# A mixture of experts after linear attention on one core: in which order two sums of the upper right product are split into high and low parts

## The chip, the cores and the metric

The kernel runs on one core of a Trainium2 chip. The metric is the device time of one execution in microseconds (us). Runs are compared by their median. The engines are named as the profile names them: PE (matmuls) with PEld (its weight loads), DVE (the vector engine), ACT (the scalar engine), POOL (GpSimd) and SP (which issues DMAs).

## What is computed

The reference is a decayed linear attention, whose output is the input of a mixture of eight experts. Cut to what matters here:

```python
state = gamma * state + einsum('bhd,bhe->bhde', k[:, :, t], v[:, :, t])
y[:, :, t] = scale * einsum('bhd,bhde->bhe', q[:, :, t], state)
x = y as rows of 512 values, 3072 of them
logits = x @ w_gate + log1p(exp(x @ w_noise)) * noise
for e in range(8):
    for k in range(2):                      # each row goes to two experts
        mask = top2[:, k] == e
        h = np.maximum(x[mask] @ w1[e], 0.0)
        out[mask] += top2_w[mask, k, None] * (h @ w2[e])
```

## The kernel before

The attention comes first (some 115 us), then the experts, one after the other. This document is about the experts 1 to 7, counted in the order in which they run (expert 0 is treated otherwise). Each has a table of slots for its rows (tokens): 832 for the experts 1 to 3, 800 for 4 and 5, 768 for 6 and 7. Every fp32 value is held as two fp16 values, a high and a low part, so that one product takes three matmuls (high by high, high by low, low by high).

**First layer of an expert (`mm1s`).** The product of w1 (1024 features) with the rows is cut into 2 by 2 blocks, halves of the inner dimension and of features by halves of the slots, and done with seven block products in place of eight, as Strassen and Winograd do. A block product is made for 128 features at a time: six matmuls over half of the slots (416, 400 or 384 columns). Such a piece is called a slot of the program, and `mm1s` counts them 0 to 27 (`slot[0]`; to keep them apart from the table's slots, they are "pieces" from here on). Pieces 0 to 11 make the first half of the features (`i = 0`), pieces 12 to 25 the second, with the last two products of the first half at 14 and 15, and 26 and 27 close. What lies in PSUM after a piece is taken up by one of three helpers:

- `kept` (L911): ACT copies it to a tile s1, s2 or s5 in SBUF. The matmuls that add to the same bank afterwards wait for that copy: piece 17 (S2 by T2) adds to the bank of piece 12, so it waits for the copy of piece 12.
- `added` (L915): DVE adds a bank to such a tile. When both of its 128 features are in (`u` is 1), `parts` follows.
- `parts` (L907, L908): ACT writes the high part (with the Relu) at once, and DVE writes the low part one piece later, out of the list `wait`.

s1 is the product's first slots (`n0 == 0`), s2 and s5 the other slots (`n0 == half`). s2 is the upper right block. Its last sum comes with piece 10 of the first half and with piece 24 of the second, that of s1 one piece later, with 11 and 25. The pieces are in program order on every engine, and an engine's queue keeps that order. Between the pieces `hook` puts other work into the queues: at pieces 5, 7, 9 and 11 ACT's high parts of w2 (`w_hi`, L214), at 6, 8, 10 and 12 DVE's low parts of w2 (`w_lo`, L219), at 11 the gates' scales (`out_scale`, L948 to L957, which waits for POOL's fetches of gates, L690), at 14, 16, 18 and 20 ACT's sums of squares (L190), at 26 a scale (L193, L200).

**Second layer (`second`, `mm2`).** For each block of 128 rows 24 matmuls of 512 columns (L992, L993, L994 for each of eight groups of 128 features, in order) run over h, the split features. Block 0 lies in the first slots. Its groups 2 and 3 are the last s1, so that its seventh matmul (L992, group 2) waits for the high part of s1, and its ninth (L994) for the low part of s1. The other slots are first read by block 3, 72 matmuls after the start.

```python
for u in range(2):
    product("S4", "B22", c[u], f0 + u, added(s2, u, f0, half), False)
product("A12", "B21", bank("pR"), f0 + 1, added(s1, 1, f0, 0))
```

Of the kernel before, what the change touches and what calls it, by code (L numbers as in the profile page):

```python
# [95 lines left out]
def moe_kernel(ctx, tc, qT, kT, kt, vt, noise, wgn, w1, w2, ctab, qtab, xbuf, gbuf, out):  # L96
# [143 lines left out]
    def a_part(n):  # L240
        return [WT["s" + h][:, int(n[1]) - 1] if n[0] == "S" else WT["1" + h][:, 2 * int(n[1]) + int(n[2]) - 3] for h in "hl"]
# [87 lines left out]
    for i in range(2):  # L329
        u = loads.tile([128, HP, 128], F32, name=f"U{i}", bufs=1)  # L330
# [493 lines left out]
    def part(e, tag="xr"):  # L824
        pool = work if tag == "xr" else hp
        return pool.tile([128, 2, CAP // 2], F32, name="s", tag=tag, bufs=3)[:, :, :CAPS[e] // 2]

    def b_part(e, n):
        if n[0] == "T":
            i = int(n[1]) - 1  # L830
            return XT[e][:, i, 0], XT[e][:, i, 1]
        k, m = 2 * (int(n[1]) - 1), CAPS[e] // 2
        t = m * (int(n[2]) - 1)
        return [XE[e][:, h + k:h + k + 2, t:t + m] for h in (0, KT)]
# [27 lines left out]
    def s_steps(n):  # L862

        a11, a12, a21, a22 = [a_stage(1, i, j) for i in range(2) for j in range(2)]
        if n == "S1":
            XS["t"] = hp.tile([128, 2, 2, 512], F32, name="xt")
        t0, t1 = XS["t"][:, 0], XS["t"][:, 1]
        out, x, y, op = {"S1": (t0, a21, a22, OP.add), "S2": (t1, t0, a11, OP.subtract),
                         "S4": (t0, a12, t1, OP.subtract), "S3": (t1, a11, a21, OP.subtract)}[n]
        hi, lo = a_part(n)  # L870
        sc = ST["1", 1][2][:, 0:1]
        return (lambda: nc.vector.tensor_tensor(out, x, y, op=op),
                lambda: nc.scalar.activation(hi, out, AF.Copy, scale=sc),
                lambda: nc.vector.scalar_tensor_tensor(lo, out, sc, hi, op0=OP.mult, op1=OP.subtract))

    def mm1s(e, hook):

        slot = [0]
        wait = []
        half = CAPS[e] // 2  # L880

        def flush():
            while wait:
                wait.pop(0)()

        def product(a, b, p, f, then, start=True):
            (ah, al), (bh, bl) = a_part(a), b_part(e, b)
            p = p[:, :half]
            for k in range(2):
                wh, wl = [w[:, k, f * 128:(f + 1) * 128] for w in (ah, al)]  # L890
                nc.tensor.matmul(p, wh, bh[:, k, :], start=start and k == 0, stop=False, skip_group_check=True)  # L891
                nc.tensor.matmul(p, wh, bl[:, k, :], start=False, stop=False, skip_group_check=True)  # L892
                nc.tensor.matmul(p, wl, bh[:, k, :], start=False, stop=(k == 1), skip_group_check=True)  # L893
            todo = list(wait)
            del wait[:]
            then(p)
            for w in todo:
                w()
            hook(slot[0])
            slot[0] += 1  # L900

        def bank(tag):
            return psum.tile([128, 512], F32, name="pH", tag=tag, bufs=2 if tag == "pA" else 1)

        def parts(src, fs, n0):
            hi, lo = [h[:, fs, n0:n0 + half] for h in (hh, hl)]
            nc.scalar.activation(hi, src, AF.Relu)  # L907
            wait.append(lambda: nc.vector.scalar_tensor_tensor(lo, src, 0.0, hi, op0=OP.max, op1=OP.subtract))  # L908

        def kept(s, u):  # L910
            return lambda p: nc.scalar.activation(s[:, u], p, AF.Copy)  # L911

        def added(s, u, f0, n0):
            def then(p):
                nc.vector.tensor_tensor(s[:, u], p, s[:, u], op=OP.add)  # L915
                if u:
                    parts(s, slice(f0, f0 + 2), n0)
            return then

        last = []  # L920
        for i in range(2):
            f0 = 2 * i
            A, Cc = [("pA", "pA"), ("pX", "pU")][::1 - 2 * i]
            a = [bank(t) for t in A]
            s1, s2, s5 = [part(e) for _ in range(3)]
            for u in range(2):
                product("A11", "B11", a[u], f0 + u, kept(s1, u))
            for u, (q, f) in enumerate(last):
                product("A22", "T4", q, f, lambda p, f=f: parts(p, 4 + f, 0), False)
            product("A12", "B21", bank("pR"), f0, added(s1, 0, f0, 0))  # L930
            for u in range(2):
                product("S2", "T2", a[u], f0 + u, kept(s2, u), False)
            c = [bank(t) for t in Cc]
            for u in range(2):
                product("S1", "T1", c[u], f0 + u, kept(s5, u))
            for u in range(2):
                product("S3", "T3", a[u], f0 + u, added(s5, u, 4 + f0, half), False)
            for u in range(2):
                product("S4", "B22", c[u], f0 + u, added(s2, u, f0, half), False)
            product("A12", "B21", bank("pR"), f0 + 1, added(s1, 1, f0, 0))  # L940
            last = [(a[u], f0 + u) for u in range(2)]
        for q, f in last:
            product("A22", "T4", q, f, lambda p, f=f: parts(p, 4 + f, 0), False)
        flush()
# [158 lines left out]
    s2, s4, s3 = s_steps("S2"), s_steps("S4"), s_steps("S3")  # L1103
# [81 lines left out]
    for e in range(1, E):  # L1185
        more = e + 1 < E

        def hook(s):
            if s == 3:
                own_tail()  # L1190
            if e == 1 and s < 3:
                xs1(1)
            n = s - 4
            if n == 0:
                w_scale(e, "2")
            if n in (1, 3, 5, 7):
                w_hi(e, "2", n // 2)
            if n in (2, 4, 6, 8):
                w_lo(e, "2", n // 2 - 1)
            if s == 11:  # L1200
                out_scale(e, 0, len(blocks(e)))
            if more:
                if 2 <= s < 9:
                    ahead(e + 1, ((6, 0, 3, 1, 4, 2, 5)[s - 2],))
                if s in (14, 16, 18, 20):
                    w_sum(e + 1, "1", s // 2 - 7)
                if s == 26:
                    w_scale(e + 1, "1")

        mm1s(e, hook)  # L1210
        for n, t in enumerate(blocks(e)):
            if more:
# [129 lines left out]
```

## Time and profile before

| | us |
|---|---|
| median of 3 runs | 650.31 (650.27 to 653.07) |
| the profiled execution, its own time | 646.82 |
| its span, first to last instruction | 645.0 |
| between the two, outside the span | 1.82 |
| granted TensorE clock, mean over the span | 0.994 of 2.4 GHz |

The profile is of one execution, whose own time is 3.49 us under the median of the timed runs. The table gives the whole; where in it the change acts is read from the trace: the timeline (instructions in order of time, with the idle time of the engine before each and what ended it) at the middle and the end of each `mm1s`.

### The profile page before, as it was taken

The page shows a single profiled execution, that of the slowest core. Times are in us where ns is not written, and L with a number is a line of the kernel's source. Part 1 is how long each engine was busy: PE and PEld are TensorE (multiplying, and loading weights), DVE is VectorE, ACT ScalarE, POOL GpSimd, SP SyncE. Part 2 cuts the span into 40 slices and gives each one's busy share as a digit, 9 for nine tenths or more (in the row PEclk, how much of TensorE's full clock was granted, in tenths as well). Part 3 has the DMA queues.
Part 4 walks back from the last instruction along what each step waited for, and adds up shares of the span by engine and source line. Part 5 has one row for each costly group of instructions (what it writes and reads, how often), then busy time and mean ns, then how long its engine had stood idle before and what let it go on. Part 6 is the DMA issues. An engine that isn't in the chain of part 4 may idle for free.

```text
span 645.0 us, 12857 instructions
## 1 busy us (share of the span) xinstructions
PE 620.2 (96%) x4949; PEld 385.9 (60%) x4949; DVE 447.8 (69%) x947; ACT 393.0 (61%) x655; POOL 396.0 (61%) x279
## 2 busy tenths in 40 slices
PE   8999998899989999999999999999999999999995
PEld 5888887656746544654465446544654465445784
DVE  5668987577758798378937983798369746967730
ACT  4787977753446775576557655775576567656311
POOL 3556998244668844784588358736773686485164
PEclk9999999899999999999999999999999999999998
DMA  9999999953976596459745964695469646943043
GB/s 318 345 373 407 373 382 337 310 192 91 168 106 160 98 262 175 47 108 232 200 52 117 227 183 53 105 259 164 51 112 245 163 49 119 232 44 40 7 53 44
DMA packets 107392, 112.88 MB, mean 175 GB/s; under 512 B 64512, under 2 KB 84224, under 8 KB 103744
## 3 DMA queue, kind: packets, MB, share of 16 engines
q1 hardware_dynamic: 86080, 84.29, 44.3%
q0 software_dynamic: 20528, 26.90, 26.6%
q8 instruction: 40, 0.66, 0.4%
q10 hardware_dynamic: 720, 0.84, 0.4%
q14 instruction: 24, 0.20, 0.1%
HBM read 72.16 MB, written 26.47 MB: 153 GB/s over the span
## 4 chain that ended last, share of the span: by engine, by line
PE 77%; DVE 9%; DMA 4%; ACT 3%; issue 3%; POOL 2%; SPq 2%; another core or an unknown queue 0%; POOLq 0%; DVEq 0%; ACTq 0%
PE pO L994 10%; PE pO L992 10%; PE pO L993 10%; PE pH L891 9%; PE pH L893 9%; PE pH L892 9%; PE pA L366 3%; PE pY L379 3%; PE pY L385 2%; DMA xe<-xg 2%; PE pX L419 2%; PE pO L983 2%; PE pO L981 1%; PE pO L982 1%; DVE h L908 1%
## 5 line engine op out<-in xcount | busy, mean ns | idle before, releaser
L968 POOL DMA_INDIRECT out<-ot,idx x108 | 196.2, 1816 | 148.1 <-ACT ot L962 60.7
L994 PE MATMUL pO<-w2h,h 128*128 128x512 f16 x336 | 127.4, 379 | 2.3 <-DVE h L908 2.0
L992 PE MATMUL pO<-w2h,h 128*128 128x512 f16 x336 | 127.4, 379 | 2.0 <-ACT h L818 1.7
L993 PE MATMUL pO<-w2l,h 128*128 128x512 f16 x336 | 127.3, 379 | 0.0
L915 DVE TENSOR_TENSOR s<-pH,s 128x416 f32<-128x416 f32 (+2 forms) x84 | 47.4, 572 | 50.0 <-PE pH L893 28.2
L690 POOL DMA_INDIRECT gx<-gbuf,idx x54 | 60.0, 1111 | 27.8 <-issue 13.1
L680 POOL DMA_INDIRECT xg<-xbuf,idx x55 | 59.4, 1080 | 23.1 <-issue 15.4
L190 ACT ACTIVATE junk<-wst 128x1024 bf16<-128x1024 f32 x64 | 67.8, 1060 | 0.0
L907 ACT ACTIVATE h<-s 128x832 f16<-128x832 f32 (+2 forms) x42 | 36.4, 873 | 42.9 <-DVE s L915 26.8
L962 ACT ACTIVATE ot<-pO,gse 128x512 f32<-128x512 f32 (+2 forms) x48 | 32.6, 681 | 44.5 <-PE pO L994 40.1
L911 ACT ACTIVATE s<-pH 128x416 f32<-128x416 f32 (+2 forms) x84 | 40.3, 509 | 31.5 <-PE pH L893 30.4
L994 PEld LDWEIGHTS <-h 128*128 128x128 f16 x336 | 32.9, 98 | 44.4 <-DVE h L908 4.4
L992 PEld LDWEIGHTS <-h 128*128 128x128 f16 x336 | 32.9, 98 | 41.4 <-ACT h L818 2.0
L891 PE MATMUL pH<-xt,wsh 128*128 128x416 f16 (+2 forms) x168 | 56.0, 333 | 0.2 <-DVE h L908 0.2
L893 PE MATMUL pH<-xt,wsl 128*128 128x416 f16 (+2 forms) x168 | 56.0, 333 | 0.0
L892 PE MATMUL pH<-xt,wsh 128*128 128x416 f16 (+2 forms) x168 | 56.0, 333 | 0.0
L993 PEld LDWEIGHTS <-h 128*128 128x128 f16 x336 | 32.9, 98 | 38.3
L849 ACT ACTIVATE xt<-s 128x832 f16<-128x832 f32 (+2 forms) x28 | 24.5, 874 | 35.3 <-DVE s L848 35.0
L219 DVE SCALAR_TENSOR_TENSOR w2l<-wst,wsc,w2h 128x1024 f16<-128x1024 f32 x28 | 35.8, 1278 | 14.1 <-ACT w2h L214 12.1
L339 POOL TENSOR_TENSOR vp<-in_v,ct 128x512 f32<-128x512 f32 x24 | 25.1, 1046 | 29.6 <-issue 10.3
L908 DVE SCALAR_TENSOR_TENSOR h<-s,h 128x832 f16<-128x832 f32 (+2 forms) x42 | 41.3, 990 | 1.0 <-ACT h L907 0.8
L373 DVE TENSOR_TENSOR am<-pA,ct 128x512 f32<-128x512 f32 x48 | 30.8, 683 | 15.4 <-PE pA L366 12.8
(216 smaller groups left out, 1489.6 us busy)
## 6 DMA issues: line engine op xcount, KB each, us to landing
wst<-w SPq DMA_DIRECT2D x28, 1024.0 KB
in_q<-qT SPq DMA_DIRECT2D x24, 256.0 KB
in_k<-kT SPq DMA_DIRECT2D x24, 256.0 KB
in_v<-vt SPq DMA_DIRECT2D x24, 256.0 KB
xbuf<-xr SPq DMA_DIRECT2D x24, 256.0 KB
out<-zero SPq DMA_DIRECT2D x12, 512.0 KB
in_kt<-kt SPq DMA_DIRECT2D x20, 256.0 KB
wst<-w SPq DMA_DIRECT2D x8, 512.0 KB
```

The lines of the kernel that those rows point to most:

```text
L190: nc.scalar.activation(junk, st[:, i * 1024:(i + 1) * 1024], AF.Square, accum_out=ss[:, i:i + 1])
L680: nc.gpsimd.indirect_dma_start(out=x[:p1], out_offset=None, in_=xbuf[:128 + rows], in_offset=bass.IndirectOffsetOnAxis(ap=idx[:p1, i:i + 1 ...
L690: nc.gpsimd.indirect_dma_start(out=GX[e][:, t, :], out_offset=None, in_=gbuf[:128 + rows], in_offset=bass.IndirectOffsetOnAxis(ap=idx[:, i ...
L891: nc.tensor.matmul(p, wh, bh[:, k, :], start=start and k == 0, stop=False, skip_group_check=True)
L892: nc.tensor.matmul(p, wh, bl[:, k, :], start=False, stop=False, skip_group_check=True)
L893: nc.tensor.matmul(p, wl, bh[:, k, :], start=False, stop=(k == 1), skip_group_check=True)
L908: wait.append(lambda: nc.vector.scalar_tensor_tensor(lo, src, 0.0, hi, op0=OP.max, op1=OP.subtract))
L915: nc.vector.tensor_tensor(s[:, u], p, s[:, u], op=OP.add)
L968: nc.gpsimd.indirect_dma_start(out=out[s], out_offset=bass.IndirectOffsetOnAxis(ap=idx[:n, i:i + 1], axis=0), in_=ot[:n, s * HD:(s + 1) * ...
L992: nc.tensor.matmul(p, a, WT["2h"][:, f, :], start=(f == 0), stop=False)
L993: nc.tensor.matmul(p, a, WT["2l"][:, f, :], start=False, stop=False)
L994: nc.tensor.matmul(p, c, WT["2h"][:, f, :], start=False, stop=(f == FT - 1))
```

## The change

At piece 10 (and 24) the sum of s2 is no longer split at once. It is put on a list, `held`. At piece 11 (and 25) s1 is split first, and s2 right behind it: ACT's high part of s1, then that of s2, and one piece later DVE's low part of s1, then that of s2. Nothing else changes; no instruction is added or taken away.

```diff
--- before.py
+++ after.py
@@ -910,12 +910,18 @@
         def kept(s, u):
             return lambda p: nc.scalar.activation(s[:, u], p, AF.Copy)
 
-        def added(s, u, f0, n0):
+        def added(s, u, f0, n0, hold=False):
             def then(p):
                 nc.vector.tensor_tensor(s[:, u], p, s[:, u], op=OP.add)
-                if u:
+                if u and hold:
+                    held.append((s, slice(f0, f0 + 2), n0))
+                elif u:
                     parts(s, slice(f0, f0 + 2), n0)
+                    while held and n0 == 0:
+                        parts(*held.pop())
             return then
+
+        held = []
 
         last = []
         for i in range(2):
@@ -936,7 +942,7 @@
             for u in range(2):
                 product("S3", "T3", a[u], f0 + u, added(s5, u, 4 + f0, half), False)
             for u in range(2):
-                product("S4", "B22", c[u], f0 + u, added(s2, u, f0, half), False)
+                product("S4", "B22", c[u], f0 + u, added(s2, u, f0, half, True), False)
             product("A12", "B21", bank("pR"), f0 + 1, added(s1, 1, f0, 0))
             last = [(a[u], f0 + u) for u in range(2)]
         for q, f in last:
```

On ACT, at the middle of expert 2's `mm1s`. The three L907 are the high parts of s5, s2 and s1 (s_3901, s_3900 and s_3899), L214 is a high part of w2, and the two L911 at the end are the copies of pieces 12 and 13. Before:

```order
L907 ACTIVATE h2_2282<-s_3901 128x2x416
L214 ACTIVATE w2h_110<-wst2_3595,wsc2_3597 128x1024
L907 ACTIVATE h2_2282<-s_3900 128x2x416
L907 ACTIVATE h2_2282<-s_3899 128x2x416
L214 ACTIVATE w2h_110<-wst2_3595,wsc2_3597 128x1024
L911 ACTIVATE s_4051<-pH_4049 128x416
L911 ACTIVATE s_4051<-pH_4050 128x416
L907 ACTIVATE h2_2282<-pH_3897 128x416
```

Now:

```order
L907 ACTIVATE h2_2282<-s_3901 128x2x416
L214 ACTIVATE w2h_110<-wst2_3595,wsc2_3597 128x1024
L907 ACTIVATE h2_2282<-s_3899 128x2x416
L907 ACTIVATE h2_2282<-s_3900 128x2x416
L214 ACTIVATE w2h_110<-wst2_3595,wsc2_3597 128x1024
L911 ACTIVATE s_4050<-pH_4048 128x416
L911 ACTIVATE s_4050<-pH_4049 128x416
L907 ACTIVATE h2_2282<-pH_3897 128x416
```

The high parts of s2 and s1 have changed places. The L214 and the two copies stand behind both, as before.

On DVE, at the same place. L915 is the last sum of s1, L908 the low parts (of s_3900, which is s2, of s_3899, which is s1, then of a bank of piece 14), L219 a low part of w2. Before:

```order
L915 TENSOR_TENSOR s_3899<-pH_4030,s_3899 128x416
L908 SCALAR_TENSOR_TENSOR h2_2282<-s_3900,h2_2282 128x2x416
L948 TENSOR_TENSOR i2_4041<-wsc1_3191,wsc2_3597 128x1
L955 TENSOR_TENSOR gm_4044<-gx_3607,pm_2894 128x7x6
L956 TENSOR_REDUCE gsm_4045<-gm_4044 128x7
L957 TENSOR_SCALAR gse_4043<-gsm_4045,i2_4041 128x7
L908 SCALAR_TENSOR_TENSOR h2_2282<-s_3899,h2_2282 128x2x416
L219 SCALAR_TENSOR_TENSOR w2l_111<-wst2_3595,wsc2_3597,w2h_110 128x1024
L908 SCALAR_TENSOR_TENSOR h2_2282<-pH_3897,h2_2282 128x416
```

Now:

```order
L915 TENSOR_TENSOR s_3899<-pH_4029,s_3899 128x416
L954 TENSOR_TENSOR i2_4040<-wsc1_3191,wsc2_3597 128x1
L961 TENSOR_TENSOR gm_4043<-gx_3607,pm_2894 128x7x6
L962 TENSOR_REDUCE gsm_4044<-gm_4043 128x7
L963 TENSOR_SCALAR gse_4042<-gsm_4044,i2_4040 128x7
L908 SCALAR_TENSOR_TENSOR h2_2282<-s_3899,h2_2282 128x2x416
L908 SCALAR_TENSOR_TENSOR h2_2282<-s_3900,h2_2282 128x2x416
L219 SCALAR_TENSOR_TENSOR w2l_111<-wst2_3595,wsc2_3597,w2h_110 128x1024
L908 SCALAR_TENSOR_TENSOR h2_2282<-pH_3897,h2_2282 128x416
```

The low part of s2 stood ahead of the four instructions of `out_scale`; now it stands behind them and behind the low part of s1. The numbers of lines have grown by 6 from there on.

On DVE, at the end of expert 2's `mm1s`, with the last sum of s1 (into s_4051, now s_4050), the low parts and the first instruction of the next scale. Before:

```order
L915 TENSOR_TENSOR s_4052<-pH_4112,s_4052 128x416
L915 TENSOR_TENSOR s_4051<-pH_4159,s_4051 128x416
L908 SCALAR_TENSOR_TENSOR h2_2282<-s_4052,h2_2282 128x2x416
L908 SCALAR_TENSOR_TENSOR h2_2282<-s_4051,h2_2282 128x2x416
L200 TENSOR_REDUCE s1_4178<-pL_106 128x1
```

Now:

```order
L915 TENSOR_TENSOR s_4051<-pH_4112,s_4051 128x416
L915 TENSOR_TENSOR s_4050<-pH_4158,s_4050 128x416
L908 SCALAR_TENSOR_TENSOR h2_2282<-s_4050,h2_2282 128x2x416
L908 SCALAR_TENSOR_TENSOR h2_2282<-s_4051,h2_2282 128x2x416
L200 TENSOR_REDUCE s1_4178<-pL_106 128x1
```

The two low parts have changed places; nothing else moved.

## Rows read from the trace of the kernel before

**Rows 1.** The page's first part: busy time, share of the span, instructions.

```profile
PE 620.2 (96%) x4949; PEld 385.9 (60%) x4949; DVE 447.8 (69%) x947; ACT 393.0 (61%) x655; POOL 396.0 (61%) x279
```

**Rows 2.** PE's waits: engine, line, waited for; us in total, times, longest.

```profile
PE pO L994 <- DVE h L908: 2.0, 5, 0.6
...
PE pO L992 <- ACT h L907: 0.3, 1, 0.3
```

**Rows 3.** Timeline, end of expert 2: start, us, engine, line, what [idle before <-releaser].

```profile
290.76 0.95 POOL L690 DMA_INDIRECT gx<-gbuf,idx  x1 [0.30 <-issue]
...
291.83 0.59 DVE L915 TENSOR_TENSOR s<-pH,s 128x416 f32<-128x416 f32 x1 [1.69 <-PE pL L193]
...
292.33 2.08 DVE L908 SCALAR_TENSOR_TENSOR h<-s,h 128x832 f16<-128x832 f32 x2
...
292.45 0.90 ACT L907 ACTIVATE h<-s 128x832 f16<-128x832 f32 x1 [1.38 <-issue]
...
293.50 0.38 PE L992 MATMUL pO<-w2h,h 128*128 128x512 f16 x1
293.71 0.38 PE L993 MATMUL pO<-w2l,h 128*128 128x512 f16 x1
...
294.47 0.39 PE L994 MATMUL pO<-w2h,h 128*128 128x512 f16 x1 [0.37 <-DVE h L908]
```

**Rows 4.** The same, end of expert 6.

```profile
543.95 0.94 POOL L690 DMA_INDIRECT gx<-gbuf,idx  x1 [0.30 <-DVE h L908]
...
544.89 0.56 DVE L915 TENSOR_TENSOR s<-pH,s 128x384 f32<-128x384 f32 x1 [1.14 <-PE pH L893]
...
545.48 0.84 ACT L907 ACTIVATE h<-s 128x768 f16<-128x768 f32 x1 [2.73 <-DVE s L915]
...
546.34 0.56 DVE L915 TENSOR_TENSOR s<-pH,s 128x384 f32<-128x384 f32 x1 [0.89 <-PE pH L893]
```

**Rows 5.** Timeline of PE, end of expert 7.

```profile
606.63 0.27 PE L982 MATMUL pO<-w2l,h 128*128 128x256 f16 x1
606.94 0.28 PE L983 MATMUL pO<-w2h,h 128*128 128x256 f16 x1
```

**Rows 6.** Timeline, middle of expert 2.

```profile
277.18 0.95 POOL L680 DMA_INDIRECT xg<-xbuf,idx  x1 [0.31 <-issue]
...
277.66 1.01 DVE L908 SCALAR_TENSOR_TENSOR h<-s,h 128x832 f16<-128x832 f32 x1
...
277.78 0.90 ACT L907 ACTIVATE h<-s 128x832 f16<-128x832 f32 x1 [0.80 <-DVE w2l L219]
278.58 1.13 ACT L214 ACTIVATE w2h<-wst,wsc 128x1024 f16<-128x1024 f32 x1
279.62 0.91 ACT L911 ACTIVATE s<-pH 128x416 f32<-128x416 f32 x2
...
280.46 0.34 PE L891 MATMUL pH<-xt,wsh 128*128 128x416 f16 x1
```

**Rows 7.** ACT by shapes, experts 1 to 7: count, busy us, mean ns of one.

```profile
L911 ACT ACTIVATE s<-pH 128x416 f32<-128x416 f32 x36 | 17.7, 522 | 13.2 <-PE pH L893 12.2 <-issue 1.0
```

**Rows 8.** Timeline, middle of expert 4.

```profile
408.26 0.88 ACT L911 ACTIVATE s<-pH 128x400 f32<-128x400 f32 x2
...
408.85 0.33 PE L891 MATMUL pH<-xt,wsh 128*128 128x400 f16 x1
```

**Rows 9.** Timeline, middle of expert 6.

```profile
534.68 0.85 ACT L911 ACTIVATE s<-pH 128x384 f32<-128x384 f32 x2
...
535.20 0.32 PE L891 MATMUL pH<-xt,wsh 128*128 128x384 f16 x1
```

**Rows 10.** Timeline, middle of expert 1.

```profile
214.69 0.17 DVE L955 TENSOR_TENSOR gm<-gx,onef 128x7 f32<-128x7 f32 x1 [0.83 <-DMA gx<-gbuf,idx]
...
218.00 0.34 PE L891 MATMUL pH<-xt,wsh 128*128 128x416 f16 x1 [0.16 <-DVE h L908]
```

## Prediction

> **What bounds the kernel now.** I read the page first: PE is busy for 96% of the span, the other engines for 60 to 70% [rows 1]. So an edit that adds and removes no work changes the time only where PE waits. The list of PE's waits came next: in the experts 1 to 7 there is one wait that speaks of the split features, L994 for DVE's low part, 5 times, 2.0 us in all, and L992 for ACT's high part, once, 0.3 us [rows 2]. These are the matmuls of group 2 in block 0, behind the last sum of s1. The idle time shown is too small: a record of these matmuls lasts 0.38 us, while undisturbed they start 0.21 us apart (L992 at 293.50, L993 at 293.71), so each wait costs PE 0.17 us more than shown. In expert 2, L994 starts 0.76 us behind L993, a loss of 0.55 for a shown 0.37 [rows 3]. All six together: 2.3 + 6 x 0.17 = 3.3 us. That is all that a faster way from s1's last sum to its low part can win there, and 0.2 more in expert 7, where the matmuls are half as wide, 0.11 us apart, and L983 starts 0.31 behind L982 [rows 5].
>
> The timeline came last, at the two places where the change acts. It is done twice in each of seven experts: at the middle of the first layer (pieces 10 to 17) and at its end (pieces 24 to 27 and the start of the second layer).
>
> **The end of the first layer: little is won directly.** The aim on paper is that s1's low part no longer stands behind that of s2 on DVE. Look at what it waits for. In expert 2 the last sum (L915) starts at 291.83. ACT's high part of s1 follows at 292.45 and takes 0.90, to 293.35. Meanwhile DVE does the low part of s2, from 292.33; two low parts in a row take 2.08 there, 1.0 each, so that of s2 ends at 293.35, when the high part of s1 does [rows 3]. The low part of s2 was hidden by the wait for the high part. Without it DVE would idle for that 1.0 us, and s1's low part would start at the same moment. Removed: nothing. What goes behind it (low part of s2, then the scale and the low parts of groups 6 and 7) comes 1.0 us later, and ACT's high parts of groups 6 and 7 some 0.8. Group 6 is needed 12 matmuls behind the waiting one, 12 x 0.21 = 2.5 us, and the next expert's weights, whose scale is late too, a whole second layer later; both cover it. The other slots' features are read first by block 3, 72 matmuls or 15 us in.
>
> **The middle of the first layer: a new wait.** Here ACT is the engine to watch. In expert 2 it does the high part of s1 at 277.78, after 0.80 of waiting for the sum, then without a pause L214 at 278.58 and the copies of pieces 12 and 13 at 279.62 [rows 6]. The high part of s2 had been done before that, in time when ACT had nothing else. Now it stands between the high part of s1 and L214, and pushes L214 and both copies by one step of such an instruction, 278.58 - 277.78 = 0.80. A copy takes 0.52 [rows 7], so the first ends at 280.14 now and at 280.94 then. PE's piece 17 starts at 280.46, and its first matmul needs that copy [rows 6]. The cover is 0.32, less the 0.04 that passes from a copy's end to PE's start (expert 6: 534.68 + 0.48 to 535.20 [rows 9]; the 0.48 is a copy of 384 columns, estimated from 0.52 for 416 by width). PE then stands still for 0.80 + 0.04 - 0.32 = 0.52 us. For the narrower experts the step and the copy are estimated from these by width:
> - 1, 2 and 3 (416 columns): 0.52 each.
> - 4 and 5 (400): the step is 0.77, a copy 0.50; it ends at 408.26 + 0.50, and piece 17 starts at 408.85, a cover of 0.09 [rows 8]: 0.77 + 0.04 - 0.09 = 0.72 each.
> - 6 and 7 (384): piece 17 starts as the copy allows it already [rows 9], so the whole step counts: 0.74 each.
>
> Sum: 3 x 0.52 + 2 x 0.72 + 2 x 0.74 = 4.48 us.
>
> On DVE the low part of s2 moves behind `out_scale`. In expert 1 that waits for fetched gates until 214.69 [rows 10], and the low part of s2 filled that wait; it now comes behind it, and all that follows comes 1.0 later. Among it is the low part of piece 14's bank, for which piece 19 waits today, at 218.00 [rows 10]. So expert 1 loses 1.0 and not 0.52. In the other experts `out_scale` does not wait; DVE's queue then loses at most the 0.80 by which L214, and so the low weights behind it, come later, and piece 19 has the time of pieces 17 and 18 to cover that. Together: 4.48 + 0.48 = 4.96, and less the 0.2 of expert 7, whose end wait is swallowed because its PE is late by more than that: **4.8 us** is lost if the waits at the end of experts 2 to 6 stay as long as they are.
>
> **How much of that the waits at the end swallow.** PE's later arrival helps nobody at 291.83 if that release is fixed in time, and then the wait behind it shrinks by as much as PE is late. If it moves with PE, the wait stays. What ends DVE's idle 1.69 us there is unclear: the sum needs piece 25 alone, and the releaser that is named, L193, comes in PE's order a whole piece behind it [rows 3]. No row shows what it is, so I bound it: none of the 3.3 us swallowed gives +4.8, all of it +1.5. The nearest row is POOL's fetch of gates: 290.76 + 0.95 = 291.71 in expert 2, and 543.95 + 0.94 = 544.89 in expert 6, where the first late sum starts at 544.89 [rows 3, 4]; in the other three the pair fits less exactly. POOL's queue does not hang on piece 17, so the fixed end is the nearer. I take two thirds swallowed, 2.2 us: 4.8 - 2.2 = **+2.6 us**. The profiled execution would take 646.8 + 2.6 = 649.4; the median of the runs shown stands 3.5 above it, and with the same step goes from 650.3 to 652.9. That is 0.4%; a measurement of this kernel can tell 0.5%, some 3.25 us, from no change.
>
> **The rivals.**
> - *Nothing is swallowed* (0.30). The late sums are late by a fixed time behind PE's pieces, and so are late again. For it: the second late sum of expert 6 comes 1.45 behind the first [rows 4], so one release does not explain both. Against it: the fit with POOL. Then +4.8, 655.1, slower. A branch of it: in expert 2 the sum of piece 24 is on time today and would come into the late stretch with PE 0.5 later; that would cost up to another 1.45, the same distance.
> - *The new wait doesn't show* (0.10). If ACT took up the high part of s2 within time it now idles, or the copies were not on PE's way, all stays, 650.3 +- 1. Against it: the queue is in order, and ACT has no pause from 277.78 on.
> - *Faster* (0.05): ACT's high part of s2 is what holds the second late sum. In expert 6 it runs from 545.48 for 0.84, to 546.32, and the sum starts at 546.34 [rows 4]. With nothing between the two sums the second would start at 545.45, 0.89 sooner, and the waits at the end would go: -3.5 us, 646.8. It decides only if piece 17 does not wait; if that wait comes, the two together give +1.5, within the range.
> - *DVE blocked by POOL* (0.03): the moved low part, with both inputs in SBUF, meets a POOL transfer and stands still behind it. POOL's fetch lasts 0.95 [rows 6]; one such stop in each expert adds up to 7 x 0.95 = 6.7 us, of which the two pieces between 17 and 19 cover most; at worst 655.5. Against it: in expert 2 the low part of s2 starts at 277.66, while POOL's fetch runs from 277.18 to 278.13, and it takes its usual 1.01 [rows 6]. The Trainium skill, "SBUF — State Buffer", section "Who interferes with whom", says that a vector instruction with two SBUF inputs contends with a GpSimd instruction that reads SBUF, and that the second one to issue fully blocks. By that rule this start would have been held for half a microsecond; the trace does not agree for this kind of POOL instruction.
>
> **How the numbers follow.** The forecast has 0.52, and its own range is +1.5 to +3.7; the part of it above 3.25 is about a fifth. Same: 0.42 of it, the rival without the wait 0.10, a little of the others 0.03: 0.55. Slower: 0.40. Faster: 0.05. The range takes in the bounds +1.5 and +4.8, half of the rival without the wait below and the branch of the first rival above: 650.2 to 655.8; what is left out is the faster case, the other half of no wait, and the worst of the rest, under 0.2.
>
> **What would show it.** Right: in the middle of each expert the copies of pieces 12 and 13 start 0.74 to 0.80 later behind the high part of s1, piece 17 starts late by 0.5 to 0.74, named as waiting for ACT's L911; in expert 1 piece 19 waits longer for DVE's low part. At the end the low part of s1 starts right behind the high part of s1, with DVE idle before it, and not sooner after the sum. The list of PE's waits has L994 for DVE below 2.0 if part is swallowed. Wrong: piece 17 in step, or L994's wait gone with the sums of pieces 24 and 25 sooner than before; or the waits as long as ever, and the loss near 5 us.

## The result and the profile after

The changed kernel takes 654.32 us in the median of 12 runs (648.70 to 660.12), the kernel before 648.40 in 12 runs of its own (645.82 to 653.07). The ratio is 1.0067, 95% interval 1.0038 to 1.0095: slower by 4.3 us (2.5 to 6.2). The ratio leaves out the two slowest executions (659.71 and 660.12 us, at the lowest granted clock of the 12, 0.988), so it says less than the 5.9 us between the two medians. The first profiled execution of the changed kernel is the one of 659.71 us, so its span (657.9) is not compared; from it come only rows inside an expert. A second trace of the same kernel (run after_again, 649.66 us, span 647.9) gives the sums.

Engine totals of that second trace, beside [rows 1]. The counts are the same, so no work came or went. Where the loss lies these totals don't tell (PE's busy time is 1.9 us longer too, at a granted clock of 0.990 for 0.994); the waits below do:

```profile
PE 622.1 (96%) x4949; PEld 386.9 (60%) x4949; DVE 450.6 (70%) x947; ACT 392.2 (61%) x655; POOL 401.3 (62%) x279
```

PE's waits of the second trace (engine, line, waited for; us in total, times, longest), beside [rows 2]:

```profile
PE pH L891 <- DVE h L908: 3.9, 1, 3.9
...
PE pH L891 <- ACT s L911: 3.3, 7, 0.6
```

The second row is new: seven waits for ACT's copy, one in each expert. It is the first matmul of piece 17, and no other. A record lasts 0.34 us and these matmuls start 0.175 apart undisturbed, so each wait is 0.17 longer than shown: 3.3 + 7 x 0.17 = 4.5 us. The first trace has the row with the same three numbers. The row above it is expert 1's piece 19, told below. The waits of L994 (now L1000) for the low part of s1 and of L992 (now L998) for its high part have no row in this trace. They have rows in the first trace after, and longer ones in all than in [rows 2]:

```profile
PE pO L998 <- ACT h L907: 2.6, 2, 2.0
...
PE pO L1000 <- DVE h L908: 1.7, 4, 0.5
```

ACT's timeline in the middle of expert 2, first trace after, beside [rows 6] (start, us, engine, line, what [idle before <-releaser]):

```profile
285.23 1.68 ACT L907 ACTIVATE h<-s 128x832 f16<-128x832 f32 x2 [2.88 <-DVE s L915]
286.81 1.13 ACT L214 ACTIVATE w2h<-wst,wsc 128x1024 f16<-128x1024 f32 x1
287.85 0.90 ACT L911 ACTIVATE s<-pH 128x416 f32<-128x416 f32 x2
```

and PE's, the same stretch:

```profile
287.74 0.34 PE L893 MATMUL pH<-xe,w1l 128*128 128x416 f16 x1
288.40 0.34 PE L891 MATMUL pH<-xt,wsh 128*128 128x416 f16 x1 [0.33 <-ACT s L911]
```

ACT now idles 2.88 us ahead of the first high part, and then does two in a row (the "x2" of 1.68 us). The first copy starts 2.62 us behind the start of the high part of s1, where it stood 1.84 behind [rows 6]: 0.78 later. PE, which would have started piece 17 at 287.91, starts at 288.40.

DVE's timeline at the end of the first layer in expert 2, first trace after, beside [rows 3]:

```profile
298.31 0.59 DVE L915 TENSOR_TENSOR s<-pH,s 128x416 f32<-128x416 f32 x1 [0.73 <-PE pH L893]
299.07 0.59 DVE L915 TENSOR_TENSOR s<-pH,s 128x416 f32<-128x416 f32 x1 [0.17 <-PE pH L893]
300.63 1.96 DVE L908 SCALAR_TENSOR_TENSOR h<-s,h 128x832 f16<-128x832 f32 x2 [0.96 <-ACT h L907]
```

DVE idles 0.96 us for the high part of s1. The low part of s1 starts 1.56 us behind the start of the last sum and, at 1.0 us, ends 2.6 behind it. In [rows 3] it ended at 292.33 + 2.08 = 294.41, 2.58 behind the start of the sum: the same, though the last two sums start 0.76 us apart here and 2.27 apart there. What that distance does is told under the experiments.

### The profile page after: what moved, and what is told of

It is laid out like the page before. It is cut to its first block, busy times and chain, and to the rows that moved or that the text cites. A ratio compares the mean times of both kernels' runs of the same rounds, so it can differ in the third digit from the quotient of the medians.

```text
span 657.9 us, 12857 instructions
## 1 busy us (share of the span) xinstructions
PE 625.9 (95%) x4949; PEld 388.6 (59%) x4949; DVE 448.4 (68%) x947; ACT 391.8 (60%) x655; POOL 398.8 (61%) x279
## 4 chain that ended last, share of the span: by engine, by line
PE 71%; DVE 13%; ACT 5%; issue 3%; DMA 3%; POOL 2%; another core or an unknown queue 0%; SPq 0%; POOLq 0%; DVEq 0%; ACTq 0%
PE pO L1000 9%; PE pO L998 9%; PE pO L999 9%; PE pH L891 7%; PE pH L893 7%; PE pH L892 7%; PE pY L379 2%; PE pA L366 2%; PE pY L385 2%; DMA out<-ot,idx 2%; POOL out L974 2%; DVE am L373 2%; PE pT L1013 2%; ACT w2h L214 1%; ACT h L907 1%
## 5 line engine op out<-in xcount | busy, mean ns | idle before, releaser
L974 POOL DMA_INDIRECT out<-ot,idx x108 | 200.4, 1856 | 155.7 <-ACT ot L968 63.0
L998 PE MATMUL pO<-w2h,h 128*128 128x512 f16 x336 | 128.2, 382 | 2.6 <-ACT h L907 2.6
L1000 PE MATMUL pO<-w2h,h 128*128 128x512 f16 x336 | 128.2, 381 | 1.7 <-DVE h L908 1.7
L915 DVE TENSOR_TENSOR s<-pH,s 128x416 f32<-128x416 f32 (+2 forms) x84 | 47.1, 571 | 54.0 <-PE pH L893 39.8
L680 POOL DMA_INDIRECT xg<-xbuf,idx x55 | 57.7, 1049 | 25.1 <-issue 15.2
L907 ACT ACTIVATE h<-s 128x832 f16<-128x832 f32 (+2 forms) x42 | 35.2, 868 | 56.0 <-DVE s L915 46.1
L911 ACT ACTIVATE s<-pH 128x416 f32<-128x416 f32 (+2 forms) x84 | 40.2, 508 | 36.4 <-PE pH L893 33.1
L1000 PEld LDWEIGHTS <-h 128*128 128x128 f16 x336 | 33.0, 98 | 43.6 <-DVE h L908 4.1
L998 PEld LDWEIGHTS <-h 128*128 128x128 f16 x336 | 33.2, 99 | 42.5 <-ACT h L907 4.2
L908 DVE SCALAR_TENSOR_TENSOR h<-s,h 128x832 f16<-128x832 f32 (+2 forms) x42 | 40.4, 990 | 7.9 <-ACT h L907 7.9
L219 DVE SCALAR_TENSOR_TENSOR w2l<-wst,wsc,w2h 128x1024 f16<-128x1024 f32 x28 | 35.8, 1278 | 14.1 <-ACT w2h L214 10.0
```

Source lines behind the costliest of these rows:

```text
L680: nc.gpsimd.indirect_dma_start(out=x[:p1], out_offset=None, in_=xbuf[:128 + rows], in_offset=bass.IndirectOffsetOnAxis(ap=idx[:p1, i:i + 1 ...
L974: nc.gpsimd.indirect_dma_start(out=out[s], out_offset=bass.IndirectOffsetOnAxis(ap=idx[:n, i:i + 1], axis=0), in_=ot[:n, s * HD:(s + 1) * ...
L998: nc.tensor.matmul(p, a, WT["2h"][:, f, :], start=(f == 0), stop=False)
L1000: nc.tensor.matmul(p, c, WT["2h"][:, f, :], start=False, stop=(f == FT - 1))
```

## Experiments

The runs came in three groups of four. Those of a group share a chip and the runs of the kernel before. Two theories stood at first: A, that the loss is made by ACT's order in the middle of the first layer; B, that it is made at the end. A third question was what the waits at the end are, since the forecast let them swallow part of the loss.

All times in us are against the kernel before in the same group. The last four columns are from each run's one trace, worked out from the starts of PE's matmuls: what piece 17 loses in all experts (0.1, which the kernel before loses too, is given as 0); what pieces 18 to 22 of expert 1 lose; what block 0 of the second layer loses in all experts; and the time from expert 1's first matmul to the end of the span.

| run, group | ratio (95%) | us | 17 | expert 1 | block 0 | expert 1 to end |
|---|---|---|---|---|---|---|
| before, first trace | | | 0 | 0.3 | 3.6 | 448.0 |
| after, first trace | 1.0067 (1.0038 to 1.0095) | +4.3 | 4.5 | 0 | 5.2 | |
| first_half, 1 | 1.0050 (1.0005 to 1.0094) | +3.2 | 4.5 | 4.0 | 1.9 | 453.5 |
| second_half, 1 | 0.9957 (0.9923 to 0.9991) | -2.8 | 0 | 0.3 | 3.4 | 447.6 |
| low_only, 1 | 1.0034 (1.0001 to 1.0068) | +2.2 | 0 | 7.0 | 2.5 | 454.0 |
| early_hold, 1 | 0.9965 (0.9939 to 0.9991) | -2.3 | 0 | 0 | 0 | 444.2 |
| after_again, 2 | 1.0065 (1.0037 to 1.0094) | +4.2 | 4.5 | 5.7 | 0 | 452.2 |
| after_w_later, 2 | 1.0005 (0.9978 to 1.0031) | +0.3 | 0 | 5.0 | 0 | 449.3 |
| x_late, 2 | 0.9975 (0.9948 to 1.0001) | -1.6 | 0 | 5.1 | 0.2 | 447.5 |
| early_scale, 2 | 0.9900 (0.9864 to 0.9936) | -6.5 | 0 | 0 | 0 | 442.2 |
| before_again, 3 | 1.0016 (0.9983 to 1.0049) | +1.0 | 0 | 0 | 3.3 | 446.8 |
| scale_late, 3 | 1.0077 (1.0048 to 1.0106) | +5.0 | 0 | 0 | 7.8 | 450.8 |
| after_scale, 3 | 1.0048 (1.0010 to 1.0085) | +3.1 | 4.5 | 0 | 2.4 | 450.4 |
| early_scale_2, 3 | 0.9974 (0.9942 to 1.0006) | -1.7 | 0 | 0 | 1.2 | 443.6 |

**The change in the first half alone (first_half), and in the second alone (second_half).** The two edits to the changed kernel:

```diff
-                product("S4", "B22", c[u], f0 + u, added(s2, u, f0, half, True), False)
+                product("S4", "B22", c[u], f0 + u, added(s2, u, f0, half, i == 0), False)    # first_half
+                product("S4", "B22", c[u], f0 + u, added(s2, u, f0, half, i == 1), False)    # second_half
```

> The change is made in the first half of the features alone (i = 0, the middle of the first layer); the end is as before. Theory A (ACT's high part of s2 stands ahead of L214 and of the copies of pieces 12 and 13): the whole loss of the change is here. PE's piece 17 starts 0.49 us late in experts 1 to 3, 0.71 in 4 and 5, 0.79 in 6 and 7 (4.5 us in all), named as waiting for ACT's copy L911, and the time is about 4.5 us above the kernel before, 0.7%, or 2.5 to 4.5 if the waits at the end take some of it up. Theory B (the loss comes from the end, where s2's split is held behind that of s1): no more than 1 us above the kernel before.

> The change is made in the second half of the features alone (i = 1, the end of the first layer); the middle is as before. Theory A: piece 17 does not wait; at the end the low part of s1 starts where the high part of s1 ends, with DVE idle before it, and not sooner after the last sum than before. Time within 1 us of the kernel before. Theory B: 3 to 4.5 us above the kernel before. Third possibility, that the edit does at the end what it says (s1 ready sooner): 2 to 3 us below.

The half in the middle is slower by 3.2 us, the half at the end faster by 2.8. Theory B falls: the end does not lose. Added up, the halves give +0.4, and the whole change is +4.3; with intervals of these widths that is not clear of the noise, and no run here explains it. In first_half's list of waits the row of the copies reads as in the second trace after: 3.3 us, 7 times.

The gain of second_half is outside theory A's "within 1 us" at its middle, though not at its interval's end (-5.0 to -0.6). Where it can come from is seen in the traces of all runs, from the starts of the sums. With the order of before, the low part of s1 ends 2.42 to 2.58 us behind the start of the last sum when the two last sums are 1.4 us or more apart, and up to 3.02 (416 columns) when they follow each other at 0.5, for then ACT's high part of s2 and DVE's low part of s2 are both still ahead of s1's. With s2 held it is 2.41 to 2.58 in every expert of every trace (the runs with the early split apart). So the edit wins up to 0.44 us an expert at the end where the sums come close together; seven times that is 3.1 us at most. That second_half won its time there is not shown: in its own trace block 0 still loses 3.4, for 3.6 in the kernel before, and from expert 1 to the end it is 0.4 us shorter.

**Only DVE's order (low_only).** ACT's order is that of before:

```diff
-            wait.append(lambda: nc.vector.scalar_tensor_tensor(lo, src, 0.0, hi, op0=OP.max, op1=OP.subtract))
+            low = lambda: nc.vector.scalar_tensor_tensor(lo, src, 0.0, hi, op0=OP.max, op1=OP.subtract)
+            if hold:
+                held.append(low)
+                return
+            wait.append(low)
+            while held and n0 == 0:
+                wait.append(held.pop())
```

> ACT keeps its order of before (high part of s2 at pieces 10 and 24, that of s1 one piece later); only DVE's two low parts change places, in both halves. Theory A: piece 17 is in step, since nothing is added ahead of ACT's copies; what is left is expert 1, where DVE's low part of s2 moves behind the wait of out_scale, up to 0.5 us. Time within 1 us of the kernel before. Rival, that DVE's order makes the loss (the low part of a bank of piece 14, and piece 19 behind it, come 1 us later): waits of piece 19 for DVE in most experts, 3 to 5 us above the kernel before.

Piece 17 is in step in all experts, as theory A has it. The time is not within 1 us: +2.2 (0.1 to 4.4). In the trace piece 19 is late by 0.10, 0.40, 0.16 and 0.16 in experts 4 to 7, 0.8 together; in the changed kernel PE comes to piece 19 later, and this does not show. The rest is expert 1, whose pieces 19 to 22 lose 7.0 us there. DVE's timeline of low_only in expert 1:

```profile
216.84 0.17 DVE L963 TENSOR_TENSOR gm<-gx,onef 128x7 f32<-128x7 f32 x1 [5.00 <-DMA gx<-gbuf,idx]
...
217.38 1.95 DVE L910 SCALAR_TENSOR_TENSOR h<-s,h 128x832 f16<-128x832 f32 x2
219.25 1.28 DVE L219 SCALAR_TENSOR_TENSOR w2l<-wst,wsc,w2h 128x1024 f16<-128x1024 f32 x1
220.45 0.58 DVE L910 SCALAR_TENSOR_TENSOR h<-pH,h 128x416 f16<-128x416 f32 x1
```

out_scale waits 5.0 us for the fetched gates; behind it stand both low parts, the low part of w2, and only then the low part of piece 14's bank, for which piece 19 waits. In [rows 10] that wait of out_scale is 0.83. How long it is depends on how far POOL is behind PE when expert 1 is reached: the runs with out_scale at piece 11 lose 0 to 7.0 us there, and x_late, which has the order of before in the middle, 5.1. So most of the 7.0 is probably not the edit's, though no run tells the two apart. The edit adds the low part of s2, 0.94, behind the wait.

**The first 128 features of s1 split early (early_hold).** In the second half, behind second_half's edit:

```diff
+                if f0 == 2 and n0 == 0:
+                    parts(s[:, u:u + 1], slice(f0 + u, f0 + u + 1), n0)
+                    while u and held:
+                        parts(*held.pop())
+                    return
```

> Second half alone: the first 128 features of s1 are split right behind their own last sum (piece 16), so that behind piece 25 only 128 are left, in half the time each, and s2 is split behind them. 14 more instructions on ACT and on DVE over the run. If the waits of group 2 in the second layer are what the late last sum and the split behind it (0.9 us high, 1.0 us low) make, then the waits for ACT's high part and DVE's low part in block 0 are nearly gone (of some 3.3 us under 1 left) and the time is 2 to 3.5 us below the kernel before, 0.3 to 0.5%. If the late sums are late by more than the 2 us that this gives, part of the waits stays and 0 to 2 us are won.

Its list of waits has no row for block 0 in experts 1 to 7, and the time is 2.3 us lower, as expected. So the edit takes the waits at the end out of its trace, which from expert 1 to the end is 3.8 us shorter than that of before. That the timed executions pay these waits is not shown by it: second_half, with 3.4 us of them in its trace, is as fast (-2.8).

**The changed kernel again (after_again), and with the copies brought forward (after_w_later).** The second is the test of theory A that leaves the change in place. w2's last high part goes behind the copies of pieces 12 and 13, its low part to piece 16:

```diff
-            if n in (1, 3, 5, 7):
-                w_hi(e, "2", n // 2)
-            if n in (2, 4, 6, 8):
-                w_lo(e, "2", n // 2 - 1)
+            if n in (1, 3, 5, 9):
+                w_hi(e, "2", min(n // 2, 3))
+            if n in (2, 4, 6, 12):
+                w_lo(e, "2", min(n // 2 - 1, 3))
```

> The changed kernel once more, for a second trace of it. Theory A (the loss is ACT's, at the middle): piece 17 starts 0.49 us late in experts 1 to 3, 0.71 in 4 and 5, 0.79 in 6 and 7, as in the first trace; the waits at the end differ from trace to trace, since the sums there come late by 0 to 3 us. Time 2 to 4.5 us above the kernel before.

> The changed kernel, but the last high part of w2 (L214), which stands ahead of the copies of pieces 12 and 13 on ACT, is put behind them, and its low part on DVE from piece 12 to piece 16. s2 stays behind s1 everywhere. Theory A (only the copies' lateness on ACT costs): the copies come 1.04 us sooner, piece 17 is in step again in all experts, its 4.5 us are gone, and the time is within 2 us of the kernel before (ACT's backlog is 0.8 us longer than in the kernel before, and may cost 0.2 to 0.4 at piece 21 in experts 4 to 6). Rival (the order s1 then s2 itself costs, on DVE or by the late features): still 3 to 4.5 us above the kernel before.

ACT and PE in the middle of expert 2, with the copies brought forward:

```profile
278.26 1.69 ACT L907 ACTIVATE h<-s 128x832 f16<-128x832 f32 x2 [2.88 <-DVE s L915]
279.85 0.90 ACT L911 ACTIVATE s<-pH 128x416 f32<-128x416 f32 x2
280.64 1.15 ACT L214 ACTIVATE w2h<-wst,wsc 128x1024 f16<-128x1024 f32 x1
...
280.76 0.34 PE L893 MATMUL pH<-xe,w1l 128*128 128x416 f16 x1
280.94 0.34 PE L891 MATMUL pH<-xt,wsh 128*128 128x416 f16 x1
```

The two high parts still stand one behind the other, the copies follow at once, and piece 17 starts 0.18 us behind its predecessor. Theory A holds: with the order s1, s2 kept and only w2's last part put behind the copies, the ratio goes from 1.0065 to 1.0005. The small waits that were expected at piece 21 came at pieces 19 and 20 instead (0.2 us in experts 2 and 3, 0.2 to 0.6 in 4 to 7, 2.2 us in all where some 1 was expected), because the low parts of the banks of pieces 14 and 15 now wait for their high parts behind L214.

after_again also sizes the loss without any wait at the end on either side. Against x_late, of the same group, whose middle is that of before, the experts 2 to 6 are longer by 0.49, 0.49, 0.70, 0.71 and 0.74 us from first matmul to the next expert's. That is what piece 17 loses in each, to within 0.05; of the 0.79 in expert 6, 0.05 is lost in the kernel before too.

**The transposes moved (x_late).** A theory S, told in the expectation below, is about what delays the last sums. In the kernel before:

```diff
-                if 2 <= s < 9:
-                    ahead(e + 1, ((6, 0, 3, 1, 4, 2, 5)[s - 2],))
+                if 2 <= s < 5:
+                    ahead(e + 1, ((6, 0, 3)[s - 2],))
+                if 5 <= s < 9 and (1, 4, 2, 5)[s - 5] in blocks(e + 1):
+                    gather(e + 1, (1, 4, 2, 5)[s - 5])
...
                 if n == 0:
+                    for i in (1, 4, 2, 5):
+                        if i in blocks(e + 1):
+                            x_t(e + 1, i)
                     w_load(e + 1, "2", 0, 2)
```

> The kernel before, but the last four transposes of the next expert's rows (L702 on SP, 10 us in expert 2) are issued behind the first layer and not beside its pieces 19 to 27; POOL's gathers stay. Theory S (while these transposes run, the count by which PE tells DVE that a piece is done arrives late, 1 to 3 us): the sums of pieces 22 to 25 come within 0.2 us of the end of their pieces, the waits of group 2 in block 0 (3.3 us in the first trace) are nearly gone, and the time is 1 to 3.5 us below the kernel before, unless the second layer now waits for the later rows. Rival (POOL's gathers or fetches make the lateness, or something fixed to PE's place): lateness and waits as before.

There are no late sums in its trace. But neither are there in the other three traces of that group, all of which have the transposes where they were, so the run proves nothing for theory S. The end of expert 2 in after_again speaks against it, and against POOL's fetch too (SP, DVE and POOL in order of time):

```profile
290.88 6.09 SPq L702 DMA_TRANSPOSE xe<-xg  x3
...
292.56 0.59 DVE L915 TENSOR_TENSOR s<-pH,s 128x416 f32<-128x416 f32 x1 [0.39 <-PE pH L893]
293.12 1.02 DVE L908 SCALAR_TENSOR_TENSOR h<-s,h 128x832 f16<-128x832 f32 x1
...
293.37 1.60 POOL L690 DMA_INDIRECT gx<-gbuf,idx  x1 [0.30 <-DVE s L915]
...
294.07 1.19 DVE L915 TENSOR_TENSOR s<-pH,s 128x416 f32<-128x416 f32 x2
```

The sum of piece 23 starts at 292.56 in the midst of the transposes, and the two last ones start at 294.07 and half a microsecond later while the fetch runs until 294.97; none is late.

**out_scale moved, with the early split and without.** To take expert 1's wait away, in early_scale and early_scale_2 (with the early split), scale_late (the kernel before) and after_scale (the changed kernel); before_again is the kernel before once more:

```diff
-            if s == 11:
+            if s == 22:
                 out_scale(e, 0, len(blocks(e)))
```

> As the run that splits the first 128 features of s1 at piece 16, and besides the gates' scale (out_scale) goes from piece 11 to piece 22. Theory: in expert 1 piece 19 waits for DVE's low part of the bank of piece 14, which stands behind out_scale, which waits for POOL's fetches; this wait was 0.3 us in the kernel before, 4.0 and 4.5 in two of the runs so far, 0 in others, as POOL stands to PE. With the scale at piece 22 it is gone in every execution, and the time is 1 to 3 us below that run, 3 to 6 below the kernel before. Rival: what PE gains there it waits for later at another work of POOL's, and the time is that of that run.

> The kernel before, but out_scale goes from piece 11 to piece 22; s1 and s2 are as before. Theory: the wait of piece 19 in expert 1 (for DVE's low part behind out_scale, which waits for POOL's fetches) is what the kernel before loses there in most executions; it is gone, and the time is 3 to 5.5 us below the kernel before, 0.5 to 0.8%. Rival (it was the early split of s1 that won most): within 1.5 us of the kernel before.

> The changed kernel, with out_scale at piece 22. Theory A: piece 17 still starts 0.49, 0.71 and 0.79 us late, 4.5 us in all, and since no other wait in the middle is left to hide it, the time is 4 to 5 us above the run with out_scale at piece 22 and the order of before; so it lies within 1.5 us of the kernel before. Rival (part of the change's loss is DVE's low part of s2 behind out_scale): only 3 us or less above that run.

> The run with the early split of s1's first 128 features and out_scale at piece 22 once more, beside the one that has out_scale at piece 22 alone. If the waits at the end cost in ordinary executions, it lies 1 to 3 us below that one; if they belong to a few executions, within 1 us of it. Against the kernel before 5 to 7 us below, as the first time.

> The kernel before once more: a second trace of it, and a measure of how far two sets of runs of one kernel lie apart. Ratio 1.000 within its interval. Piece 17 in step in all experts. Theory S (the late sums at the end belong to some executions, not to the order of the program, since four later traces have none): no wait of group 2 for the split s1 in block 0 here, and a wait of 3 to 4 us of piece 19 in expert 1, where the changed kernel's second trace has 4.0. Rival (the waits at the end are the kernel's own): some 3.3 us of them, as in the first trace.

With the early split the move wins as expected in group 2 (-6.5), where expert 1 loses 5.0 to 5.7 us in the three other traces; in group 3, where it loses nothing, -1.7. So against the kernel before early_scale_2 missed its 5 to 7 us, and it is 6.7 below scale_late, not 1 to 3. Without the early split the expectation failed: +5.0. DVE and PE at the end of expert 2 in scale_late show where its trace loses most:

```profile
289.05 0.59 DVE L915 TENSOR_TENSOR s<-pH,s 128x416 f32<-128x416 f32 x1 [3.46 <-PE pL L193]
289.55 1.01 DVE L908 SCALAR_TENSOR_TENSOR h<-s,h 128x832 f16<-128x832 f32 x1
290.49 1.08 DVE L915 TENSOR_TENSOR s<-pH,s 128x416 f32<-128x416 f32 x2
292.03 1.96 DVE L908 SCALAR_TENSOR_TENSOR h<-s,h 128x832 f16<-128x832 f32 x2 [0.47 <-ACT h L907]
```

```profile
290.54 0.38 PE L994 MATMUL pO<-w2h,h 128*128 128x512 f16 x1
292.84 0.39 PE L992 MATMUL pO<-w2h,h 128*128 128x512 f16 x1 [1.93 <-ACT h L907]
293.07 0.38 PE L993 MATMUL pO<-w2l,h 128*128 128x512 f16 x1
294.06 0.53 PE L994 MATMUL pO<-w2h,h 128*128 128x512 f16 x1 [0.61 <-DVE h L908]
294.38 0.63 PE L992 MATMUL pO<-w2h,h 128*128 128x512 f16 x1
294.80 0.63 PE L993 MATMUL pO<-w2l,h 128*128 128x512 f16 x1
```

The sum of piece 23 is late by some 3.7 us (it starts 3.95 behind the start of piece 24, and in after_again 0.20), and those of 24 and 25 start 0.5 apart (the "x2" of 1.08): this is the close case of above, in all seven experts of this trace. Block 0 waits, and behind the waits of 1.93 and 0.61 us the matmuls start 0.43 apart, not 0.21. The table by windows gives the granted clock (window, its length, PE busy, clock, DMA share, GB/s):

```profile
289.50:292.80 3.30, 1.42 (x7) 1.00 0.98 127
292.80:296.00 3.20, 2.55 (x7) 0.71 1.27 197
296.00:299.00 3.00, 3.00 (x12) 0.74 1.27 211
```

It falls to 0.71 and 0.74 in the mean of these stretches, behind PE's two waits; the matmuls at twice the distance ran at the lower of its two levels, 1.2 GHz. Block 0 loses 7.8 us in all experts, 4.6 of it here. With s2 held (after_scale) it loses 2.4; the 5.4 between them are about what piece 17 costs, so the two traces come out alike (450.4 and 450.8 from expert 1 to the end), where theory A alone had a difference of 4 to 5. In the timed runs after_scale is at +3.1 and scale_late at +5.0, so both parts of after_scale's expectation failed. The control (before_again) is at 1.0016, and its waits at the end are there: 3.3 us, so the rival of its expectation is right for this trace.

The fastest version in both groups is that of early_scale: 638.93 us against 645.43 in its group, and 644.35 against 647.53 in the other, where the interval just reaches no change.

## Why the prediction was right, and which step was off

**The middle of the first layer: right.** The forecast had piece 17 late by 0.52, 0.72 and 0.74 us, 4.48 in all, by a step of ACT less a cover. The traces have 0.49, 0.71 and 0.79, 3 x 0.49 + 2 x 0.71 + 2 x 0.79 = 4.5, in the four traces that have the hold in the first half and w2's last part ahead of the copies; the others have 0.07 or less in any expert. Of the 0.79, 0.05 is there in the kernel before, so the change adds 0.74, as forecast. The copies came 0.78 later for 0.80 forecast. That it is this wait that costs the time is shown by after_w_later, which leaves the change as it is, moves w2's last part alone, and is back at 1.0005 (0.9978 to 1.0031).

**Expert 1: open.** The forecast gave it 1.0 and not 0.52, since the low part of s2 filled out_scale's wait. In the first trace after, the gates were there in time, and expert 1 lost 0.49 like the next two. Where out_scale waits, POOL's lag decides between nothing and 5.7 us (the two traces of the changed kernel), far more than this term; the 0.94 behind the wait is seen on DVE, but not told apart in the times.

**"Little is won directly" at the end: nearly right.** "Removed: nothing" holds where the last two sums are 1.4 us apart, as in expert 2, on which the step was worked out. Where they come close together the hold wins up to 0.44 us an expert. second_half is faster by 2.8 us (0.6 to 5.0), though its trace does not show where.

**"I take two thirds swallowed, 2.2 us": this failed.** It made +2.6 of +4.8. Measured are +4.3 (2.5 to 6.2) and, in the second set of runs, +4.2 (2.4 to 6.1): 2.6 lies at the lower end of both intervals, and the rival "nothing is swallowed", 4.8, fits better. Two readings under that step were wrong. The release of the late sums was tied to POOL's fetch from two experts of one trace; after_again has the fetch beside sums that are in time. And the waits at the end were taken for a fixed store that PE's lateness draws on: with the order of before they are 0.2 to 3.6 us in the traces (x_late, before) and 7.8 in scale_late, with s2 held 0 to 5.2 (after_again, the first trace after). In the second set of runs the trace of the changed kernel has none and so nothing to swallow, and the full 4.5 of piece 17 stand. In the first trace after they are longer than in the first of before, with PE late: that is the sign of being wrong that the forecast named, "the waits as long as ever, and the loss near 5 us" (+4.3 by the ratio). Whether PE's being late takes up a part of them in other executions is not settled: first_half, with the end as before, is at +3.2 (0.3 to 6.1) and loses 1.9 in block 0.

The time came out at 654.32, in the range of 650.2 to 655.8, and that is in part luck. The range was laid from 650.31, the median of the three runs shown; in 12 runs the kernel before is at 648.40. From there the same steps, -0.1 to +5.5, give 648.3 to 653.9: the step by the ratio, +4.3, lies in it, the median of 654.32 would not have.

**The other rivals.** The new wait did show. "Faster" needed piece 17 in step; second_half is that case, and it is faster, though by less than the 3.5 us given. No stop of DVE behind POOL was seen: none of the moved low parts took over 1.05 us.

## What to carry to other kernels

When work is moved behind other work on an in-order engine, look at what stood behind the new place: here a high part that ran in ACT's idle time was put in front of two copies that PE waits for, and the wait could be computed to a few hundredths from one step and one cover in the trace. A wait that differs from trace to trace is no store to count on; take a second look at another place of the same trace before letting it pay for a new loss. And when the end of a stage waits for its last split, splitting the part that is ready earlier can take that wait away, as in the trace of early_hold; that it wins more time than reordering what is ready last is not shown (-2.3 and -2.8 us).

## What was not expected

- In the ten traces outside group 2, DVE's sums of pieces 22 to 25 start late in most experts, though DVE is idle and PE runs in step. In the four traces of group 2 the last sum starts 0.20 to 0.40 us behind the start of piece 26 in every expert; in the others up to 4.12 behind it (expert 1 of the first trace after). Neither the transposes nor POOL's fetch alone makes it, as after_again shows. In expert 7 the last sum is in time in all fourteen traces, 0.20 to 0.28 behind the start of piece 26; it is the only one beside whose pieces nothing is fetched, transposed or scaled for a next expert. What makes the others late stays open, and so does whether it belongs to the chip, since each group ran on its own.
- A scale of four small instructions on DVE (0.15 to 0.23 us each), moved into that stretch, came with 5.0 us of loss over the run. That it makes the sums late is not shown, since they are late without it too.
- In expert 2 of scale_late the granted clock fell to 0.71 behind waits of 1.93 and 0.61 us. In expert 1 of the first trace after PE waited 2.0 us at the same matmul, and those behind it went on 0.22 apart: a wait of this length does not always bring the fall.
- Expert 1's wait for POOL's gates costs 0 to 0.3 us in some executions and 4 to 7 in others; the two traces of the changed kernel alone have 0 and 5.7.
